# A float32 attention and FFN kernel on one core: the second FFN product of chunks 4 to 6 on two levels of Strassen's scheme, weights of chunks 3 to 6 converted in chunks 2 and 3, two-term sums through PSUM copies

## The chip, the cores and the metric

The kernel runs on one core of a Trainium2 chip, one launch, all arithmetic on the device. The metric is the device time of a run in microseconds (us): 2410.17 as the median of three runs, 2409.39 to 2412.51.

## The reference, cut to what matters

Talking-heads attention is followed by a Fourier mixing layer and a two-layer FFN with a residual. Batch 8, 12 heads, 448 positions, head size 64; so 3584 tokens of 768 numbers.

```
scores = scale * q @ k^T                      # per head
scores = mix heads with w_pre; softmax over j; mix heads with w_post
x  = attn @ v                                 # (8, 448, 768)
u  = x + real(fft over tokens and features of x)
un = (u - mean(u)) / sqrt(var(u) + 1e-6)
ch = max(un @ w_ch1, 0) @ w_ch2               # (768 x 3072), then (3072 x 768)
return u + ch
```

The two FFN weights come as float64 and are turned into float32 on the device with integer operations on VectorE.

## The kernel before

The first part, attention and Fourier mixing, takes 855.6 us; the change doesn't touch its code. The second part, `ffn_phase`, is the FFN. It cuts the 3072 hidden columns into NC = 6 chunks of 512 and the 3584 tokens into NTB = 7 blocks of 512, and runs 42 passes: pass n has chunk c = n // 7 and block t = n % 7. The text counts chunks from 1 to 6, so chunk 4 starts with pass 21.

Both products of a pass are computed with one level of Strassen's scheme in Winograd's form: seven products of half-size matrices for eight. `first(n)` (from L966) does un @ w_ch1: seven products, each of 6 matmuls of 128x128 weights by 256 columns, in the order `ORDER` = 0, 4, 5, 1, 6, 2, 3. The combinations of un and of the weights are prepared ahead: those of un in `total` (L962), which stores all seven for later chunks (`ub_scr`), those of the weights by the class `_Weights`. The results are summed as they come: products 0, 5, 6 and 3 accumulate in one PSUM tile P, 4 and 2 in R, 1 in Q. Sums of two terms that lie in different tiles are made by copying the first to SBUF (ScalarE, L990 to L994) and adding the second to it (VectorE, L996, L999, L1002), with the ReLU after it on ScalarE (L997, L1000, L1003, L1005). Then come the combinations of the hidden tile h that the next product needs: `hs1` = h21 + h22 (L1020), `hs2` = hs1 - h11 (L1021), h21 = h11 - h21 (L1022).

`second(n, h)` (from L1025) multiplies h with the chunk's part of w_ch2: seven products, each of 4 matmuls (two row halves by two hidden halves) of 128x128 weights by 384 columns. In chunk 1 the sums are added to u (L1049). In later chunks they are made in an SBUF tile `od` by copies on ScalarE (L1058) and sums on VectorE (L1060), and each finished quarter is added to the output in memory by a DMA with accumulation, issued by GpSimd (L1062). h12 - hs2 is made in place after product 1 (L1065).

Matmuls are float32: the trace shows each as two records, with a weight load (LDWEIGHTS) each.

The order on TensorE and VectorE is the order of the program text (`tc.manual_schedule`); in `ffn_phase` the other engines' and the DMA queues' order is the scheduler's. [...] PSUM has two tiles for each of P, Q and R, and from pass 1 a third for P and R (`ps_tile`). h has one buffer (`ph`), the combinations of un have eleven (`pub`).

Weights of chunk c + 1 are converted during chunk c. `_Weights.add` queues a part: four pieces of seven VectorE operations each (L235 to L261), four combining sums (L267), loads (L213) and stores (L221) by GpSimd's DMA queue. `deal(k)` lets the next k VectorE operations out; it stands after the products of both functions with 3 and 4. A chunk has five parts, one each in five of its seven passes, and `deal(1000)` at the end of a pass lets out the rest. SyncE loads the converted weights (`load_w1`, `load_w2`) in the last pass of a chunk, each as soon as its buffer is free, and the next pass's un combinations (`new_ub`) through all passes.

Of the kernel before, what the change touches and what calls it, by code (L numbers as in the profile page):

```python
# [837 lines left out]
OPENS = (0, 1, 4)  # L838
DEST = {0: (0, 0), 1: (0, 0), 4: (1, 1), 5: (0, 1), 2: (0, 1), 6: (1, 1), 3: (1, 0)}
# [4 lines left out]
def ffn_phase(ctx, tc, rest, ident, u_scr, u_rev, wts, ub_scr, out, fold_rest,  # L844
# [15 lines left out]
    pw2 = pool("pw2", 7)  # L860
# [23 lines left out]
    us, ubs, w1, w2 = {}, {}, {}, {}  # L884
    pd = []
# [24 lines left out]
    def load_w2(c, i):  # L910
        w2[i] = pw2.tile([P, FM, DH], F32, name="w2t", tag="w2t")
        nc.sync.dma_start(out=w2[i][:, :, :], in_=wts.w2[c][i])
# [57 lines left out]
    def first(n):  # L970

        c, t = divmod(n, NTB)
        h = ph.tile([P, 6, FM, HT], F32, name="h", tag="h")

        h11, h12, h22, h21, hs1, hs2 = (h[:, x] for x in range(6))
        norms = c == 0 and t + 1 < NTB
        ps = {}
        for k, i in enumerate(ORDER):
            if i in OPENS:
                ps[ACC[i]] = ps_tile(ACC[i])  # L980
            p = ps[ACC[i]].rearrange("p (m t) -> p m t", m=FM)
            ub = ubs.pop((n, i))
            for m in range(FM):
                for kc in range(NK):
                    nc.tensor.matmul(p[:, m, :], w1[i][:, kc, m * P:(m + 1) * P],  # L985
                                     ub[:, kc, :],
                                     start=i in OPENS and m == kc == 0,
                                     stop=kc == NK - 1, skip_group_check=True)
            if i == 0:
                nc.scalar.copy(out=h11, in_=p)  # L990
            elif i == 4:
                nc.scalar.copy(out=h22, in_=p)
            elif i == 5:
                nc.scalar.copy(out=h21, in_=p)  # L994
            elif i == 1:
                nc.vector.tensor_tensor(h11, h11, p, op=ALU.add)  # L996
                nc.scalar.activation(h11, h11, ACTF.Relu)  # L997
            elif i == 6:
                nc.vector.tensor_tensor(h22, h22, p, op=ALU.add)  # L999
                nc.scalar.activation(h22, h22, ACTF.Relu)  # L1000
            elif i == 2:
                nc.vector.tensor_tensor(h21, h21, p, op=ALU.add)  # L1002
                nc.scalar.activation(h21, h21, ACTF.Relu)  # L1003
            else:
                nc.scalar.activation(h12, p, ACTF.Relu)  # L1005
            if norms and k < NT2:
                stats(t + 1, k)
                if k == NT2 - 1:
                    power(t + 1)
            if n == 0 and k not in (1, 2):  # L1010
                next_part()
            if i != 2:
                wts.deal(2 if norms else 3)
            if t == NTB - 1 and c + 1 < NC:
                load_w1(c + 1, i)
            if NTB <= n + 1 < NC * NTB:
                new_ub(n + 1, i)
                nc.sync.dma_start(out=ubs[n + 1, i][:, :, :],
                                  in_=ub_scr[(n + 1) % NTB][i])
        nc.vector.tensor_tensor(hs1, h21, h22, op=ALU.add)  # L1020
        nc.vector.tensor_tensor(hs2, hs1, h11, op=ALU.subtract)  # L1021
        nc.vector.tensor_tensor(h21, h11, h21, op=ALU.subtract)  # L1022
        return h

    def second(n, h):  # L1025
        c, t = divmod(n, NTB)
        h11, h12, h22, hs3, hs1, hs2 = (h[:, x] for x in range(6))
        lhs = (h11, h12, h12, h22, hs1, hs2, hs3)
# [7 lines left out]
        for k, i in enumerate(ORDER):  # L1036
            for x in range(NT2 // 2):
                if i in OPENS:
                    ps[ACC[i], x] = ps_tile(ACC[i])
                p = ps[ACC[i], x][:, :DH]  # L1040
                for kf in range(FM):
                    nc.tensor.matmul(p, lhs[i][:, kf, x * P:(x + 1) * P],  # L1042
                                     w2[i][:, kf, :], start=i in OPENS and kf == 0,
                                     stop=kf == FM - 1, skip_group_check=True)
                r, d = DEST[i]
                last = i in (1, 6, 2, 3)
                if c == 0:
                    us_ = u[:, 2 * r + x, d * DH:(d + 1) * DH]
                    nc.vector.tensor_tensor(us_, us_, p, op=ALU.add)  # L1049
                    if last:  # L1050
                        r0 = t * TB + (2 * r + x) * P
                        nc.sync.dma_start(out=acc[t, r, d][:, x, :], in_=us_)
                    continue
                if (r, d) not in os:
                    os[r, d] = pd[0].tile([P, 2, DH], F32, name="od", tag="od")
                o = os[r, d][:, x, :]
                if i in (0, 4, 5, 3):
# [6 lines left out]
            if i == 1:  # L1064
                nc.vector.tensor_tensor(h12, h12, hs2, op=ALU.subtract)  # L1065
# [8 lines left out]
            wts.deal(2 if norms and k >= NT2 else 4)  # L1074
            if t == NTB - 1 and c + 1 < NC:
                load_w2(c + 1, i)
# [11 lines left out]
    with tc.manual_schedule(engines={ET.PE, ET.DVE}):  # L1088
# [7 lines left out]
        for n in range(NC * NTB):  # L1096
            c, t = divmod(n, NTB)

            if c + 1 < NC and 0 <= t - (c == 0) < NK + FM:
                wts.add(c + 1, t - (c == 0))  # L1100
            wts.deal(0)
            if c == 0 and t + 2 < NTB:
                load_u(t + 2)
            second(n, first(n))
            wts.deal(1000)
            if n == 0:
                assert not parts
                rest.close()
                pd.append(pool("pd", 6, side="right"))
                beside.close()  # L1110
                pps.append(pool("ppy", space=bass.MemoryType.PSUM))

# [60 lines left out]
```

## Time and profile before

| | |
|---|---|
| median of three runs | 2410.17 us (2409.39 to 2412.51) |
| the profiled execution | 2417.4 us, its span 2415.6 us |
| first pass starts | at 855.6 us |
| pass 0; passes 1 to 5 | 49.1 us; 39.9 us each |
| passes 6 to 40 | 36.19 us each: 18.13 us first product, 18.06 us second |
| from the last pass's second product to the end of the span | 26.8 us |
| DMA share in chunks 2 to 5; chunk 6 | 0.73 to 0.74; 0.54 |

A row of the profile gives line, engine, operation, operands with shape, number, busy time and the mean of one in ns. Records of pipelined matmuls overlap, so a row's mean (379 ns for 128x256) is longer than the distance between two of them (216 ns); where pace matters, the starts are read. PEld is the weight load. A part of the trace is asked for by a window in us from the start of the span.

### The profile page before, as it was taken

To read this page: it belongs to the slowest core of one execution; us is meant where nothing else is said; L and a number is where in the kernel's file an instruction comes from. 1 tells how busy PE (TensorE), PEld (TensorE's weight loads), DVE (VectorE), ACT (ScalarE), POOL (GpSimd) and SP (SyncE) were. 2 spreads that over 40 slices of the span, in tenths; PEclk is the share of its full clock that TensorE was granted. 3 is DMA by queue.
4 is the path that set the end of the run, shared out by engine and by line. 5 is a ranking of instruction groups with operands and counts; after the bars stand their busy time and mean duration, and the time that the engine had idled before them with its cause. 6 is when DMAs were issued, how large, how long until landed. Compare 5 with 4: busy or idle time off the path is not lost.

```text
span 2415.6 us, 55276 instructions
## 1 busy us (share of the span) xinstructions
PE 2363.0 (98%) x21680; PEld 1592.6 (66%) x21680; DVE 1408.6 (58%) x2859; ACT 932.7 (39%) x2335; POOL 960.3 (40%) x1395
## 2 busy tenths in 40 slices
PE   6999999999999999999999999999999999999998
PEld 2555555555555577677777777777777777777775
DVE  3888888888887767775555255624552455421221
ACT  4777777666667532231222222222222222222221
POOL 3587877868776541210223023212222223111111
PEclk9999999999999999999999999999999999999999
DMA  7565555655554565658687677777686777585453
GB/s 160 163 179 167 183 172 166 190 162 180 169 164 157 165 248 184 213 180 308 165 198 187 182 201 171 197 184 201 173 205 149 221 190 188 137 232 112 108 115 53
DMA packets 207184, 427.59 MB, mean 177 GB/s; under 512 B 38990, under 2 KB 128870, under 8 KB 206926
## 3 DMA queue, kind: packets, MB, share of 16 engines
q1 hardware_dynamic: 129902, 261.60, 32.4%
q0 software_dynamic: 71456, 161.08, 31.1%
q8 instruction: 173, 2.83, 0.5%
q10 hardware_dynamic: 5568, 1.38, 0.4%
q14 instruction: 85, 0.70, 0.1%
HBM read 211.98 MB, written 129.39 MB: 141 GB/s over the span
## 4 chain that ended last, share of the span: by engine, by line
PE 77%; issue 11%; DMA 4%; DVE 2%; POOL 2%; ACT 1%; SPq 1%; POOLq 0%; ACTq 0%; DVEq 0%
PE psP L985 15%; PE psP L1042 14%; PE psR L985 7%; PE psR L1042 7%; PE mx L486 6%; PE ms L459 5%; PE ms L547 5%; PE po L520 5%; PE psQ L1042 4%; PE psQ L985 4%; DMA Kr<-Sb 3%; POOL out_dram L1062 2%; PE ms L661 2%; PE ms L434 1%; SPq L475 1%
## 5 line engine op out<-in xcount | busy, mean ns | idle before, releaser
L985 PE MATMUL psP<-ub,w1t 128*128 128x256 f32 x2016 | 462.5, 379 | 0.0
L1042 PE MATMUL psP<-w2t,h 128*128 128x384 f32 x1344 | 460.9, 486 | 0.0
L985 PEld LDWEIGHTS psP<-ub,w1t 128*128 128x128 f32 x2016 | 382.8, 190 | 60.7
L1062 POOL DMA_DIRECT2D out_dram<-od x140 | 170.9, 1221 | 590.5 <-DVE od L1060 467.7
L1042 PEld LDWEIGHTS psP<-w2t,h 128*128 128x128 f32 x1344 | 254.4, 190 | 165.9
L510 POOL TENSOR_SCALAR PP<-PP,rcp 128x448 f32<-128x448 f32 x384 | 253.8, 670 | 230.0 <-DVE rcp L508 201.2
L500 ACT ACTIVATE PP<-mx,nmx 128x448 f32<-128x448 f32 x384 | 240.7, 632 | 174.4 <-DVE nmx L493 162.9
L493 DVE TENSOR_REDUCE nmx<-mx 128x1 f32<-128x448 f32 x384 | 223.0, 617 | 94.4 <-PE mx L486 92.5
L213 POOL DMA_DIRECT2D raw<-in_moe_w_ch_dram x120 | 72.6, 605 | 515.1 <-DVE tmp L257 507.7
L1058 ACT COPY od<-psP 128x384 f32<-128x384 f32 x210 | 100.6, 479 | 437.1 <-PE psP L1042 437.1
L486 PE MATMUL mx<-Kr,kw 60*32 60x448 f32 x3072 | 236.4, 552 | 17.2 <-DMA Kr<-Sb 13.7
L996 DVE TENSOR_TENSOR h<-h,psQ 128x512 f32<-128x512 f32 x42 | 28.9, 687 | 381.3 <-PE psQ L985 381.3
L985 PE MATMUL psR<-ub,w1t 128*128 128x256 f32 x1008 | 231.3, 379 | 0.0
L1042 PE MATMUL psR<-w2t,h 128*128 128x384 f32 x672 | 230.5, 486 | 0.0
L531 DVE STREAM_TRANSPOSE Pv<-po 128x896 f32<-128x896 f32 x192 | 212.6, 1107 | 9.0 <-PE po L520 6.1
L520 PE MATMUL po<-PP,kw 60*32 60x448 f32 x3072 | 214.2, 543 | 3.4 <-POOL PP L510 1.8
L459 PE MATMUL ms<-kT,qT 64*32 64x448 f32 (+1 forms) x3072 | 207.2, 547 | 7.3 <-ACT qT L330 6.4
L985 PEld LDWEIGHTS psR<-ub,w1t 128*128 128x128 f32 x1008 | 191.4, 190 | 25.9
L330 ACT COPY Sb<-ms 124x448 f32<-124x448 f32 x384 | 184.0, 542 | 36.7 <-DMA Kr<-Sb 16.1
L547 PEld LDWEIGHTS ms<-Pv,vv 64*64 64x64 f32 x5376 | 144.5, 133 | 70.5 <-issue 37.3
L1042 PEld LDWEIGHTS psR<-w2t,h 128*128 128x128 f32 x672 | 127.2, 190 | 87.4
L547 PE MATMUL ms<-Pv,vv 64*64 64x120 f32 x5376 | 167.8, 269 | 1.0 <-issue 1.0
(101 smaller groups left out, 2925.0 us busy)
## 6 DMA issues: line engine op xcount, KB each, us to landing
ub<-ub SPq DMA_DIRECT2D x294, 384.0 KB
Kr<-Sb SPq DMA_DIRECT2D x768, 105.0 KB
out_dram<-od POOLq DMA_DIRECT2D x140, 384.0 KB, 6.3
raw<-in_moe_w_ch_dram POOLq DMA_DIRECT2D x72, 256.0 KB, 3.8
raw<-in_moe_w_ch_dram POOLq DMA_DIRECT2D x48, 384.0 KB, 3.7
w<-wst POOLq DMA_DIRECT2D x126, 128.0 KB, 3.5
w<-wst POOLq DMA_DIRECT2D x84, 192.0 KB, 3.5
w1t<-w SPq DMA_DIRECT2D x42, 384.0 KB
```

Source lines behind the costliest of these rows:

```text
L330: (nc.scalar.copy if eng == "a" else nc.vector.tensor_copy)(out=out, in_=in_)
L459: nc.tensor.matmul(pss[x][o:o + hi - lo, :S], st["qT", xx][64 * x:64 * x + 64, y, lo:hi], st["kT", xx][64 * x:64 * x + 64, y, :], start=Tr ...
L486: nc.tensor.matmul(mx[x][64 * z + o:64 * z + o + 32, :S], kw1[64 * x:64 * x + KR, o:o + 32], Kr[64 * x:64 * x + KR, z, :], start=True, sto ...
L493: nc.vector.tensor_reduce(nmx[:, :], steps[T]["mx"][x][:, :S], axis=AX.X, op=ALU.max, negate=True)
L500: nc.scalar.activation(steps[T]["PP"][:, x, :], steps[T]["mx"][x][:, :S], ACTF.Exp, bias=steps[T]["nmx", x][:, :], accum_out=steps[T]["den ...
L510: nc.gpsimd.tensor_scalar(PP[:, x, :], PP[:, x, :], rcp[:, x:x + 1], 1.0, op0=ALU.mult, op1=ALU.mult)
L520: nc.tensor.matmul(po[o:o + 32, z, :S], kw2[64 * z:64 * z + KR, y, :], PP[64 * z:64 * z + KR, :, c * HS:(c + 1) * HS], start=True, stop=True)
L531: nc.vector.transpose(g["Pv"][:, T % GT, :].rearrange("p (z s) -> p z s", z=2), steps[T]["po"][:, :, :S])
L547: nc.tensor.matmul(pss[y][64 * x:64 * x + 64, :nu * R], st["v", pr][64 * y:64 * y + 64, x, jb * D:(jb + 1) * D], _ap(Pv, 64 * y * rp + 32 ...
L985: nc.tensor.matmul(p[:, m, :], w1[i][:, kc, m * P:(m + 1) * P], ub[:, kc, :], start=i in OPENS and m == kc == 0, stop=kc == NK - 1, skip_g ...
L1042: nc.tensor.matmul(p, lhs[i][:, kf, x * P:(x + 1) * P], w2[i][:, kf, :], start=i in OPENS and kf == 0, stop=kf == FM - 1, skip_group_check ...
L1062: nc.gpsimd.dma_start(out=acc[t, r, d], in_=os[r, d][:, :, :], accum_op=ALU.add)
```

## The change

In chunks 4 to 6 (`DEEP` = 3), `second` is replaced by `second2`: each of its seven products (256 x 256 by 256 x 384) is again made of seven, on 128 x 128 weights by 192 columns, 49 matmuls in all. The combinations of the left side are made by `quarter`: for h11 and h22, and for h12 and h12 - hs2, on GpSimd, for h21, hs1 and hs2 on VectorE; those of the right side by `halves`, once in a chunk, in turn on VectorE and GpSimd. The matmuls of three neighbouring products are interleaved by steps: product j starts at step 7j, and its matmuls m = 0, 4, 5, 1, 6, 2, 3 stand at 0, 3, 4, 5, 8, 13 and 16 after it. Steps from 49 on run among the next pass's first product (`SEAM`), and the first matmul of step 0 runs before the last two matmuls of `first`. ScalarE takes results out of PSUM (`take`) and copies a first term into another PSUM tile (`begin`), where the second is accumulated by the matmul without its start flag. VectorE adds (`more`) and joins products (`both`); each output quarter leaves by one DMA with accumulation, and in the last pass one quarter by two. In chunks 4 to 6 ScalarE's and GpSimd's order is that of the text too.

In `first` from pass 9 on, and in `second` from chunk 2 on, the sum of products 0 and 1 is made the same way, by a ScalarE copy of P into Q. h12 - hs2 has its own place in h and is made before the second product. The weights of chunks 3 and 4 are converted in chunk 2, those of 5 and 6 in chunk 3, and unfinished conversions of these chunks go on into the next pass. w2 has a buffer for each of the seven products, `od` seven buffers for six.

```diff
+ORDER2 = (0, 3, 5, 6, 4, 1, 2)
+DEEP = 3
+CONV = ((1, 2, 3), (2, 4, 5))
...
-    pw2 = pool("pw2", 7)
+    pw2 = pool("pw2")
...
+    H11, H22, H21, HS1, HS2, H12, H12S = range(7)
+    LHS = (H11, H12, H12S, H22, HS1, HS2, H21)
...
+    def quarter(eng, hq, h, f0, f1, s):
+        o = hq[:, f0:f1, :, :]
+        a11, a12, a21, a22 = (h[:, f0:f1, f, x * P:(x + 1) * P]
+                              for x in range(2) for f in range(2))
+        to, a, b, op = ((o[:, :, 0], a21, a22, ALU.add),
+                        (o[:, :, 1], o[:, :, 0], a11, ALU.subtract),
+                        (o[:, :, 2], a11, a21, ALU.subtract),
+                        (o[:, :, 3], a12, o[:, :, 1], ALU.subtract))[s]
+        eng.tensor_tensor(to, a, b, op=op)
+    def halves(i, eng):
+        wt[i] = right["wt"].tile([P, 3, DQ], F32, name="wt", tag=f"wt{i}")
+        b11, b12 = w2[i][:, 0, :DQ], w2[i][:, 0, DQ:]
+        b21, b22 = w2[i][:, 1, :DQ], w2[i][:, 1, DQ:]
+        t1, t2, t4 = (wt[i][:, x, :] for x in range(3))
+        for to, a, b in ((t1, b12, b11), (t2, b22, t1), (b12, b22, b12), (t4, b21, t2)):
+            eng.tensor_tensor(to, a, b, op=ALU.subtract)
...
+        deep = c >= DEEP
+        seed = n >= NTB + 2
...
+            if deep and t == 0:
+                halves(ORDER2[k], (nc.vector, nc.gpsimd)[k % 2])
...
+                    for fn in beside.pop(done, ()):
+                        fn()
+                    done += 1
...
-                                     start=i in OPENS and m == kc == 0,
+                                     start=i in (0, 4, 1)[:3 - seed] and m == kc == 0,
...
+            if i == 0 and seed:
+                ps["Q"] = ps_tile("Q")
+                nc.scalar.copy(out=ps["Q"][:, :], in_=ps["P"][:, :])
...
+            elif i == 1 and seed:
+                nc.scalar.activation(h11, p, ACTF.Relu)
...
+                if deep:
+                    for x in range(4):
+                        quarter(nc.gpsimd, hq, h, H11, H22 + 1, x)
...
+            if i == 2:
+                vec.tensor_tensor(hs1, h21, h22, op=ALU.add)
+                vec.tensor_tensor(hs2, hs1, h11, op=ALU.subtract)
+                vec.tensor_tensor(h21, h11, h21, op=ALU.subtract)
+                if deep:
+                    for x in range(4):
+                        quarter(vec, hq, h, H21, HS2 + 1, x)
...
-        nc.vector.tensor_tensor(hs1, h21, h22, op=ALU.add)
-        nc.vector.tensor_tensor(hs2, hs1, h11, op=ALU.subtract)
-        nc.vector.tensor_tensor(h21, h11, h21, op=ALU.subtract)
-        return h
-    def second(n, h):
+        vec.tensor_tensor(h12s, h12, hs2, op=ALU.subtract)
+        if deep:
+            for x in range(4):
+                quarter(nc.gpsimd, hq, h, H12, H12S + 1, x)
...
-                if i in (0, 4, 5, 3):
+                if i == 0:
+                    q = ps["Q", x] = ps_tile("Q")
+                    nc.scalar.copy(out=q[:, :DH], in_=p)
+                elif i in (4, 5, 1, 3):
...
-            if i == 1:
-                nc.vector.tensor_tensor(h12, h12, hs2, op=ALU.subtract)
...
+    def second2(n, st):
+        c, t = divmod(n, NTB)
...
+        def mm(j, m):
+            i = ORDER2[j]
+            h, hq = st["h"][:, LHS[i]], st["hq"][:, LHS[i]]
+            key = {0: "P", 5: "P", 6: "P", 3: "P", 4: "R", 2: "R", 1: "Q"}[m]
+            if m in (0, 4):
...
+            a = {0: h[:, 0, :P], 1: h[:, 1, :P], 3: h[:, 1, P:], 4: hq[:, 0], 5: hq[:, 1],
+                 6: hq[:, 2], 2: hq[:, 3]}[m]
+            b = {0: w2[i][:, 0, :DQ], 1: w2[i][:, 1, :DQ], 2: w2[i][:, 1, DQ:],
+                 3: wt[i][:, 2], 4: wt[i][:, 0], 5: wt[i][:, 1], 6: w2[i][:, 0, DQ:]}[m]
+            nc.tensor.matmul(ps[j, key][:, :DQ], a, b, start=m in (0, 4), stop=True,
+                             skip_group_check=True)
...
+        def take(j, q, key):
+            nc.scalar.copy(out=part(j, q), in_=ps[j, key][:, :DQ])
+        def begin(j):
+            ps[j, "Q"] = ps_tile("Q")
+            nc.scalar.copy(out=ps[j, "Q"][:, :DQ], in_=ps[j, "P"][:, :DQ])
+        def more(j, q, key):
+            vec.tensor_tensor(part(j, q), part(j, q), ps[j, key][:, :DQ], op=ALU.add)
+        def both(eng, j, k):
+            eng.tensor_tensor(D[j][:, :, :], D[j][:, :, :], D[k][:, :, :], op=ALU.add)
+        def out_(j, r, d):
+            nc.gpsimd.dma_start(out=acc[t, r, d], in_=D[j][:, :, :], accum_op=ALU.add)
...
+        for j, i in enumerate(ORDER2):
+            b = 7 * j
+            for s, m, q, key in ((0, 0, None, None), (3, 4, 3, "R"), (4, 5, 1, "P"),
+                                 (5, 1, None, None), (8, 6, None, None),
+                                 (13, 2, None, None), (16, 3, 2, "P")):
+                on(b + s, mm, j, m)
+                if m == 0:
+                    on(b + s, begin, j)
+                if key:
+                    on(b + s, take, j, q, key)
+            on(b + 6, take, j, 0, "Q")
+            on(b + 11, more, j, 3, "P")
+            on(b + 16, more, j, 1, "R")
             if t == NTB - 1 and c + 1 < NC:
-                load_w2(c + 1, i)
+                on(b + 17, load_w2, c + 1, i)
+        j0, j3, j5, j6, j4, j1, j2 = range(7)
+        for j, ops in ((j5, ((j5, j0),)), (j6, ((j6, j5), (j3, j6))),
+                       (j4, ((j6, j4), (j5, j4))), (j1, ((j0, j1),))):
+            for o in ops:
+                on(7 * j + 19, both, vec, *o)
+        on(7 * j6 + 20, out_, j3, 1, 0)
+        on(7 * j4 + 20, out_, j6, 1, 1)
+        on(7 * j1 + 20, out_, j0, 0, 0)
+        if n < NC * NTB - 1:
+            on(7 * j2 + 19, both, vec, j5, j2)
+            on(7 * j2 + 20, out_, j5, 0, 1)
+        else:
+            on(7 * j4 + 20, out_, j5, 0, 1)
+            on(7 * j2 + 19, out_, j2, 0, 1)
+        return at
...
+        parts_ = [(0, 1, k) for k in range(NK + FM)]
+        parts_ += [(c, d, k) for c, *ds in CONV for d in ds for k in range(NK + FM)]
+        for n in range(DEEP * NTB):
             c, t = divmod(n, NTB)
-            if c + 1 < NC and 0 <= t - (c == 0) < NK + FM:
-                wts.add(c + 1, t - (c == 0))
+            for _ in range((0 < t < NK + FM + 1) if c == 0 else 2 if t < 3 else 1):
+                if parts_ and parts_[0][0] == c:
+                    wts.add(*parts_.pop(0)[1:])
...
+            if c == 0 or t == NTB - 1:
+                wts.deal(1000)
...
+    SEAM = {49: 0, 50: 1, 51: 1, 52: 1, 53: 2, 54: 2, 55: 3, 56: 3, 57: 4, 58: 5, 59: 5}
+    with tc.manual_schedule(engines={ET.PE, ET.DVE, ET.Activation, ET.Pool}):
+        rest_ = {}
+        for n in range(DEEP * NTB, NC * NTB):
+            st = {}
+            at = second2(n, st)
+            beside = {}
+            for s_ in sorted(rest_):
+                beside.setdefault(SEAM.get(s_, s_ - 54), []).extend(rest_[s_])
+            beside.setdefault(NK * FM * 7 - 2, []).extend(at.pop(0))
+            first(n, st, beside)
+            rest_ = {}
+            for s_ in sorted(at):
+                if s_ < 49:
+                    for fn in at[s_]:
+                        fn()
+                else:
+                    rest_[s_] = at[s_]
```

## The prediction

> Passes are numbered 0 to 41: chunk 1 holds 0 to 6, chunks 4 to 6 hold 21 to 41. Times are us unless marked ns.
>
> **What bounds the kernel now.** I read the page, the windows by pass, then the timelines of single passes.
>
> ```profile
> span 2415.6 us, 55276 instructions
> PE 2363.0 (98%) x21680; PEld 1592.6 (66%) x21680; DVE 1408.6 (58%) x2859; ACT 932.7 (39%) x2335; POOL 960.3 (40%) x1395
> ```
> ```profile
> 1393.50:1429.70 36.20, 36.20 (x141) 26.60 (x140) 18.94 (x47) 8.08 (x15) 11.18 (x15) 1.00 0.72 194
> ...
> 1574.50:1610.70 36.20, 36.20 (x142) 26.61 (x141) 7.98 (x13) 8.08 (x15) 4.79 (x4) 1.00 0.57 127
> 1610.70:1646.80 36.10, 36.10 (x141) 26.55 (x140) 9.55 (x18) 8.08 (x15) 4.81 (x4) 1.00 0.88 248
> ```
> TensorE is bound. After each window stand length, then busy PE, PEld, DVE, ACT and POOL, clock, DMA share, GB/s. In passes 14, 19 and 20 PE is busy throughout at full clock; the others are far from full. Pass 14 converts weights, 19 doesn't, 20 loads the next chunk's.
>
> A busy PE proves little, so I check its pace:
> ```profile
> 1662.38 2.75 PE L985 MATMUL psP<-ub,w1t 128*128 128x256 f32 x12
> 1664.97 2.74 PE L1042 MATMUL psP<-w2t,h 128*128 128x384 f32 x8
> 1667.55 2.74 PE L1042 MATMUL psR<-w2t,h 128*128 128x384 f32 x8
> ```
> Products start 2.59 and 2.58 apart: 12 records of 215.8 ns, 8 of 322.5. A float32 matmul has two records, each with a weight load. A pass is 18.13 + 18.06 = 36.19, and passes 6 to 40 all start 36.19 apart: no bubble to save. Only less PE work helps.
>
> **What the Trainium skill says.** "TensorE: Matmul & The Clock Gate", section Back-to-back issue gap: N/2.4 + 2.5 ns. With two passes over the columns in a record it gives 215.8 and 322.5 ns, as the trace has; for N = 192 it gives 162.5. Its section LDWEIGHTS says columns/1.2, so 107 ns for 128. The trace agrees:
> ```profile
> 889.87 0.82 PE L952 MATMUL psQ<-ident,un 128*128 128x128 f32 x6
> 890.52 1.48 PE L661 MATMUL ms<-tcs,z 97*113 97x193 f32 x8
> 891.83 2.74 PE L1042 MATMUL psQ<-w2t,h 128*128 128x384 f32 x8
> ```
> Six transposes with 128 weight columns in 0.65: 108 ns each. Eight records of 192 or 193 columns in 1.31: 164 ns. So weight loads hide under narrow matmuls too, though the row of a load shows 190 ns.
>
> "SBUF — State Buffer", section Who interferes with whom: a VectorE instruction with two SBUF inputs and a GpSimd one that reads SBUF exclude each other for the whole instruction. The trace agrees:
> ```profile
> L267 DVE TENSOR_TENSOR wst<-wst x120: 404/426/2728, 164.7 to 2075.2; 128x256 f32<-128x256 f32 x72, 128x384 f32<-128x384 f32 x48
> L615 POOL TENSOR_TENSOR xq<-xs x64: 579/594/1304, 138.1 to 861.5; 113x192 f32<-113x192 f32 x32, 113x191 f32<-113x191 f32 x32
> ```
> The 2728 ns of L267 (minimum/median/maximum) lie where GpSimd ran sums back to back.
>
> "PSUM — Partial Sum Buffer", The four PSUM rules: a ScalarE write leaves the accumulate bits alone, so a matmul adds onto a copied seed where an earlier matmul set the bit. No trace here shows that; it touches the result, not the time.
>
> **Part 1, second product on two levels, passes 21 to 41.** 28 matmuls of 384 columns go, 49 of 192 come: 98 x 162.5 ns = 15.93 for 56 x 322.5 = 18.06. Gain 2.13 a pass, 44.8 in 21.
>
> New side work in a pass. ACT: 35 copies of 192 columns at 0.32 (L1058 479 ns for 384, L330 211 for 60), with the first product's some 15.5 of 34.1. DVE: fourteen 192-column sums at 0.355, seven `both` at 0.95 (L964), `quarter` four at 0.55, six 512-column sums at 0.69: 18. POOL: eight `quarter` sums of 256 columns at 0.73 (between L615 594 ns for 192 and L601 1001 for 384), four output DMAs at 1.21: 10.7. None is full, so it is a question of order. In the steady part each wait has slack: a small product's m=6 follows its m=5 by four matmuls (1.30), while m=5's own 0.33, 0.20 until ACT sees its end, the copy of 0.32 and 0.16 to restart make 1.0. DVE falls 0.3 behind at the double `both` and the waiting m=3 has over 0.8.
>
> **Part 2, the turn from first to second product.** Put 0 at the end of `first`'s last matmul. The product i=2 ended at -2.92 (after it come six wide matmuls of 0.43 and one narrow of 0.33). The chain after it is in pass 41 of the trace:
> ```profile
> 2386.38 0.69 DVE L1002 TENSOR_TENSOR h<-h,psR 128x512 f32<-128x512 f32 x1 [1.83 <-PE psR L985]
> 2387.10 0.63 ACT L1003 ACTIVATE h<-h 128x512 f32<-128x512 f32 x1 [1.89 <-DVE h L1002]
> 2387.76 0.69 DVE L1020 TENSOR_TENSOR h<-h 128x512 f32<-128x512 f32 x1 [0.70 <-ACT h L1003]
> 2388.49 0.69 DVE L1021 TENSOR_TENSOR h<-h 128x512 f32<-128x512 f32 x1
> ...
> 2389.10 0.68 DVE L1022 TENSOR_TENSOR h<-h 128x512 f32<-128x512 f32 x1
> ```
> From i=2's end (2386.18) to the end of L1022 is 3.61: now at +0.69. Behind it on DVE stand four `quarter` (two dependent, 0.03 gaps; two overlapping by 0.08: to 2.79), `h12s` (to 3.40) and only then the first `more` (3.31 to 3.67). For that sum waits m=3 of the first small product, the twelfth matmul: due at 11 x 0.325 = 3.58. Behind it on PE is everything. A matmul that waited for L959's copy began 0.05 after it and lost 0.10 of prefetch, so it runs at 3.83: bubble 0.25. Then the port: POOL's `quarter` of H11 and H22 runs from -3.81 to -0.86 (i=6 ends at -5.51, sum and relu of H22 by -3.89, then four of 0.73), and DVE's `hs1`, due at -1.33, has two SBUF inputs. It waits 0.47, of which some 0.12 overlaps its start: +0.35. I take 0.6 a pass: 12.6 (bounds 0.25 to 0.8: 5 to 17).
>
> In the first pass of chunks 4, 5, 6 `halves` comes too: four DVE sums of 0.35 ahead of `h12s` (1.2) and four on POOL right behind `quarter`, which hold the port against `hs1` and `hs2` for up to 2.4. I take 3.5 x 3 = 10.5 (0 to 12).
>
> **Part 3, conversions moved.** Chunks 2 and 3 carry two chunks' worth each: 46 operations dealt a pass instead of 32, dealt as densely as before, but with no rest. DVE: 46 at about 0.45 = 20.5 and 6.3 of sums, 27 of 36.2. Its sums are early in either half, with over 1 us to spare before PE needs P again. Each raw load and wst store moves along, on POOL's queue among the output DMAs: 5.8 x 0.6 + 10 x 0.6 + 4 x 1.21 = 14. DMA: a part costs 0.18 of a pass's share (0.74 mean with, 0.57 without); 1.44 parts make 0.83, but passes 13 and 20 also load weights (+0.31): 1.14, that is 5 us too much. `ub` loads are issued a pass early, so I cost this at 1 (0 to 8; without that cover 5 each). In chunks 5 and 6 DVE and queues are relieved, which PE didn't wait for: nothing.
>
> In pass 20 DVE's order puts the first `halves` ahead of that pass's own sums; they wait for w2 loads, which are issued as the products end, the fifth at 13 of `second`, and take some 4 (the 384 KB raw loads land after 3.7). Sums due at 13 come at about 17, and PE's i=3, due at 15.5, waits: 3 (0 to 6; below nothing excluded, since nothing is removed there).
>
> **Part 4, sums by PSUM copies.** An ACT copy at i=0 is used two products later; the DVE sum at i=1 goes. PE waits for neither: 0.
>
> **Part 5, the tail.** Now the last DMA is issued 1.0 after the last matmul ends:
> ```profile
> 2407.81 1.19 POOL L1062 DMA_DIRECT2D out_dram<-od  x1 [1.24 <-ACT od L1058]
> ```
> and lands 6.1 later. After, the last two DMAs add to the same block, so the second waits for the first (issued near 17 of `second2`, after the last double `both`, landing at 23); it lands at 29 to 30. With 1.6 after it: 31, where before 26.8 followed `second`'s start. Pass 41's 2.13 is in the gain already, so the cost is the tail's growth from 8.7 to 14: 5 (3 to 6).
>
> **Sum.** 44.8 - 12.6 - 10.5 - 1 - 3 - 5 = 12.7. The profiled execution, 2417.4 (span 2415.6), would become 2404.7; it lies 7.2 above the median of the runs. On the median, 2410.2 - 12.7 = 2397.5.
>
> **Rivals.**
> A, the forecast: 2397.5, own range 2388 to 2405. Chance 0.45.
> B, the port costs nothing, the turn only 0.25 and 1.2: 44.8 - 5.3 - 3.6 - 5 = 31: 2379. For it: overlaps of L261 with GpSimd in which it still took 404 ns. Against: `quarter` reads two SBUF inputs, as the rows that blocked did. 0.25.
> C, chunks 2 and 3 pay: raw loads late behind output DMAs, DVE stalls, passes 13 and 20 lose 5 each: 2407. Against: 36.19 a pass at 0.88 DMA share. 0.17.
> D, slower: POOL's `quarter` is longer than I think. Each us past -0.86 goes one for one into the turn. At 1.0 a sum (L601's) it ends at +0.25, the bubble is 1.7, 36 in all, with 19.5 of the rest: 2421. It decides from a bubble of 1.2. Against: L615 and L601 bracket 256 columns. 0.10.
> E, weight loads don't hide: 98 x 190 ns = 18.6, more than before: 2430 or more. Against: 108 ns. 0.03.
>
> About 0.2% (4.8) can be told from no change. Faster: A, B and a little of C, 0.75; within: 0.12; slower: D, E, 0.13. The range reaches from B to beyond C: 2377 to 2409.
>
> **What would show it.** Passes 21 to 40 start about 34.7 apart (B 34.3, D over 36); narrow records 162 to 164 ns; in each pass one PE gap some 3.5 after `first`, ended by a 192-column DVE sum into od; `hs1` some 0.35 longer than 688 ns; passes 21, 28, 35 longest; passes 7 to 19 still 36.19; the last DMA some 6 after the one before it. Wrong if PE waits for ACT throughout `second2`, or if passes 7 to 20 stretch.

## The result, and the profile after

| | before | after |
|---|---|---|
| median of the runs (us) | 2410.17 (11 runs, 2404.54 to 2419.14) | 2399.41 (11 runs, 2391.20 to 2406.53) |
| profiled execution (span) | 2417.4 (2415.6) | 2406.5 (2404.8) |
| start of pass 0 in the profile | 855.57 | 854.16 |
| from there to the end | 1560.05 | 1550.60 |

The ratio is 0.9958, 95% interval 0.9941 to 0.9974: faster, by 10.8 us on the medians where 12.7 was forecast. All that stands ahead of pass 0 is the same code in every kernel here, and takes 844 to 856 us from one profiled run to the next. So I compare what follows the first matmul of pass 0: 9.45 less. That is one profiled execution against one; the medians come from 11 runs each.

The page of after, PE first. It is still busy for almost the whole span, with less work to do:
```profile
span 2404.8 us, 58524 instructions
PE 2325.9 (97%) x22562; PEld 1703.2 (71%) x22562; DVE 1601.5 (67%) x3244; ACT 1090.0 (45%) x2930; POOL 1107.1 (46%) x1600
```
Four passes of after as windows: 15, 20, 22 and 28. The columns are the length, busy PE, PEld, DVE, ACT and POOL, the clock, the DMA share and GB/s.
```profile
1429.83:1466.02 36.19, 36.19 (x141) 26.60 (x140) 22.68 (x57) 8.96 (x17) 12.04 (x18) 1.00 0.78 196
1610.78:1651.70 40.92, 38.16 (x142) 27.33 (x141) 27.85 (x66) 8.96 (x17) 10.53 (x16) 0.96 0.96 304
1687.44:1722.14 34.70, 34.47 (x184) 31.83 (x183) 17.06 (x32) 15.00 (x43) 10.61 (x13) 1.00 0.55 126
1895.70:1932.78 37.08, 34.48 (x185) 31.81 (x183) 26.19 (x48) 14.99 (x43) 19.16 (x25) 1.00 0.54 141
```
Pass 15 converts weights for two chunks and still takes 36.19. Pass 20, the last of chunk 3, takes 4.7 more. Pass 22 is what a deep pass (one with `second2`) costs, 34.70; pass 28, a first pass of a chunk, has 2.4 more, and DVE and POOL are each 9 busier in it. PE is busy throughout in pass 15 and nearly so in 22; no other engine is near full in any of the four; in pass 20 the DMA share is 0.96.

The starts of all passes, taken from the first matmul of each, give this list (36.19 is the length before). Passes 22 to 27, 29 to 34 and 36 to 40 are the 17 ordinary deep passes.

| passes | length after (us) |
|---|---|
| 6 to 13, 15 to 19 | 36.19 |
| 14 | 37.74 |
| 20 | 40.91 |
| 21 | 35.75 |
| 22 to 27, 29 to 34, 36 to 40 | 34.69 to 34.75 |
| 28, 35 | 37.08, 38.54 |
| 41 to the end | 51.73 (before: 44.98) |

The pace inside the second product, from the timeline of pass 22. Each row is one matmul of 192 columns, two records:
```profile
1716.94 0.49 PE L1149 MATMUL psQ<-w2t,h 128*128 128x192 f32 x2
1717.27 0.49 PE L1149 MATMUL psR<-w2t,hq 128*128 128x192 f32 x2
1717.59 0.49 PE L1149 MATMUL psP<-w2t,h 128*128 128x192 f32 x2
```
They start 0.325 apart, 162.5 ns a record: TensorE follows its own pace there, and no weight load shows.

The turn from the first to the second product in pass 24, timeline of DVE, POOL and PE:
```profile
1773.68 0.73 POOL L985 TENSOR_TENSOR hq<-hq,h 128x256 f32<-128x256 f32 x1
...
1773.88 0.69 DVE L1046 TENSOR_TENSOR h<-h,psR 128x512 f32<-128x512 f32 x1 [1.80 <-PE psR L1021]
...
1775.05 0.75 POOL L985 TENSOR_TENSOR hq<-h,hq 128x256 f32<-128x256 f32 x1
1775.27 1.08 DVE L1059 TENSOR_TENSOR h<-h 128x512 f32<-128x512 f32 x1 [0.70 <-ACT h L1047]
1776.38 0.69 DVE L1060 TENSOR_TENSOR h<-h 128x512 f32<-128x512 f32 x1
...
1779.71 0.68 DVE L1071 TENSOR_TENSOR h<-h 128x512 f32<-128x512 f32 x1
...
1780.31 0.35 DVE L1165 TENSOR_TENSOR od<-od,psP 128x192 f32<-128x192 f32 x1
...
1780.71 0.59 PE L1149 MATMUL psP<-wt,h 128*128 128x192 f32 x2 [0.23 <-DVE od L1165]
```
`hs1` (L1059) starts while POOL's last quarter sum runs and takes 1.08 where `hs2`, of the same form, takes 0.69. The sum just before it (L1046), whose second input lies in PSUM, runs beside POOL sums of the same kind for its whole length and loses nothing: 0.69. At the end of the chain the matmul waits for the first `more` (L1165). By the starts of the records, TensorE's gap there is 0.39, and the next record starts 0.10 later than its pace; this second part is called restart below.

### The profile page after: what moved, and what is told of

The parts are those of the page before. It is cut to its first block, busy times and chain, and to the rows that moved or that the text cites. A ratio compares the mean times of both kernels' runs of the same rounds, so it can differ in the third digit from the quotient of the medians.

```text
span 2404.8 us, 58524 instructions
## 1 busy us (share of the span) xinstructions
PE 2325.9 (97%) x22562; PEld 1703.2 (71%) x22562; DVE 1601.5 (67%) x3244; ACT 1090.0 (45%) x2930; POOL 1107.1 (46%) x1600
## 4 chain that ended last, share of the span: by engine, by line
PE 79%; DVE 7%; DMA 6%; issue 3%; ACT 2%; POOL 1%; SPq 1%; POOLq 0%; DVEq 0%; ACTq 0%
PE psP L1021 15%; PE psR L1021 9%; PE psP L1093 8%; PE mx L486 6%; PE psP L1149 6%; PE ms L459 5%; PE ms L547 5%; PE po L520 5%; PE psQ L1021 4%; PE psR L1093 4%; PE psR L1149 3%; DMA Kr<-Sb 3%; PE psQ L1093 2%; DVE hq L985 2%; PE ms L661 2%
## 5 line engine op out<-in xcount | busy, mean ns | idle before, releaser
L1021 PE MATMUL psP<-ub,w1t 128*128 128x256 f32 x2016 | 475.9, 379 | 1.3 <-DVE h L1040 1.3
L510 POOL TENSOR_SCALAR PP<-PP,rcp 128x448 f32<-128x448 f32 x384 | 254.7, 673 | 229.2 <-DVE rcp L508 199.9
L1093 PE MATMUL psP<-w2t,h 128*128 128x384 f32 x672 | 232.3, 489 | 2.8 <-DVE od L1113 2.8
L1171 POOL DMA_DIRECT2D out_dram<-od x85 | 103.1, 1230 | 213.4 <-ACT od L1158 161.4
L1040 DVE TENSOR_TENSOR h<-h,psP 128x512 f32<-128x512 f32 x42 | 28.9, 687 | 252.1 <-PE psP L1021 251.8
L985 POOL TENSOR_TENSOR hq<-h 128x256 f32<-128x256 f32 x84 | 61.4, 731 | 276.3 <-issue 170.6
L1093 PEld LDWEIGHTS psP<-w2t,h 128*128 128x128 f32 x672 | 127.4, 191 | 85.1 <-DVE od L1113 3.7
L1168 DVE TENSOR_TENSOR od<-od 128x768 f32<-128x768 f32 x146 | 137.6, 954 | 35.3 <-ACT od L1158 34.3
L221 POOL DMA_DIRECT2D w<-wst x210 | 129.1, 648 | 50.6 <-DVE wst L267 22.3
```

The costliest lines, as they stand in the source:

```text
L510: nc.gpsimd.tensor_scalar(PP[:, x, :], PP[:, x, :], rcp[:, x:x + 1], 1.0, op0=ALU.mult, op1=ALU.mult)
L1093: nc.tensor.matmul(p, h[:, LHS[i], kf, x * P:(x + 1) * P], w2[i][:, kf, :], start=i in (0, 4, 1)[:3 - (c > 0)] and kf == 0, stop=kf == FM ...
```

## Experiments

Each kernel is the changed kernel with one edit, unless said otherwise. "From pass 0" is the time from its first matmul to the end of the span in the profile; after has 1550.60. Each ratio is to the kernel before in the same session, from 4 to 20 runs.

| kernel | median | ratio to before, 95% | from pass 0 |
|---|---|---|---|
| h12s behind the first `more` | 2387.4 | 0.9902 (0.9879 to 0.9925) | 1538.80 |
| POOL's quarter off `hs1` | 2387.9 | 0.9920 (0.9892 to 0.9947) | 1540.33 |
| one POOL sum twice | 2412.0 | 1.0004 (0.9994 to 1.0015) | 1565.70 |
| halves earlier | 2390.8 | 0.9920 (0.9893 to 0.9947) | 1539.86 |
| conversions and copies alone | 2411.8 | 1.0002 (0.9987 to 1.0016) | 1563.34 |
| halves pinned behind pass 20 | 2396.4 | 0.9946 (0.9933 to 0.9959) | 1544.27 |
| conversions dealt faster | 2395.0 | 0.9944 (0.9922 to 0.9965) | 1542.85 |
| one DMA at the end | 2398.6 | 0.9949 (0.9937 to 0.9962) | 1548.23 |
| four edits | 2374.9 | 0.9859 (0.9835 to 0.9883) | 1524.08 |
| five edits | 2376.1 | 0.9846 (0.9823 to 0.9870) | 1522.31 |
| five, and the relu later | 2379.9 | 0.9865 (0.9843 to 0.9887) | 1526.63 |

My theory is the forecast's: the turn is DVE's order and the shared port, and the single losses are places where DVE or POOL has something put ahead. The rivals were that the port costs nothing, that chunks 2 and 3 pay for the conversions, and that another engine ends at the same time, so that nothing is gained.

### DVE's order at the turn

```diff
-        vec.tensor_tensor(h12s, h12, hs2, op=ALU.subtract)
-        if deep:
-            for x in range(4):
-                quarter(nc.gpsimd, hq, h, H12, H12S + 1, x)
+        if not deep:
+            vec.tensor_tensor(h12s, h12, hs2, op=ALU.subtract)
...
+        def late():
+            h = st["h"]
+            vec.tensor_tensor(h[:, H12S], h[:, H12], h[:, HS2], op=ALU.subtract)
+            for x in range(4):
+                quarter(nc.gpsimd, st["hq"], h, H12, H12S + 1, x)
...
+        on(12, late)
```
Step 12 lies behind the first `more`, at step 11.

> Edit: in chunks 4 to 6 the sum h12s and POOL's four quarter sums of H12 and H12S are issued after the first 192-column DVE sum (more) of the second product instead of before it; nothing is left out. Theory A (DVE's order makes the turn): h12s stood ahead of that sum with a pitch of 0.60 us, and the gap was 0.39 + 0.10, so an ordinary deep pass falls from 34.70 to 34.2 apart, the gap of some 2.74 in passes 21, 28 and 35 falls by 0.60, and the whole by 18 x 0.49 + 3 x 0.60 = 10.6. Rival (TensorE waits there for something else that ends at the same time: ScalarE's copies or GpSimd): passes stay at 34.70 and the time does not move.

Passes 22 to 27, 29 to 34 and 36 to 40 are 34.20 apart, 0.50 less; pass 28 fell by 0.60 to 36.48. From pass 0 it is 11.8 less where 10.6 was expected; 1.2 of that is pass 20, which no part of the edit touches and which takes 39.6 to 42.8 in the kernels that leave it as it is. The timeline of pass 24 of this kernel:
```profile
1770.31 0.35 DVE L1163 TENSOR_TENSOR od<-od,psP 128x192 f32<-128x192 f32 x1
1770.57 0.68 DVE L1173 TENSOR_TENSOR h<-h 128x512 f32<-128x512 f32 x1
...
1770.93 0.49 PE L1147 MATMUL psP<-wt,h 128*128 128x192 f32 x2
```
The sum that TensorE needs (L1163) now runs ahead of `h12s` (L1173), and the matmul has no wait. `h12s` itself is needed six small products later. So the gap is DVE's order; the rival, another engine that ends at the same time, falls.

### The shared port

```diff
             elif i == 1 and seed:
                 nc.scalar.activation(h11, p, ACTF.Relu)
+                if deep:
+                    for x in range(4):
+                        quarter(nc.gpsimd, hq, h, H11, H11 + 1, x)
...
-                        quarter(nc.gpsimd, hq, h, H11, H22 + 1, x)
+                        quarter(nc.gpsimd, hq, h, H22, H22 + 1, x)
```


> Edit: POOL's four quarter sums over H11 and H22 together (256 columns, 0.73 each, which overlap DVE's hs1) become four of H11 alone right after its relu and four of H22 alone after its relu (128 columns each); h12s stays where it is; nothing is left out. Theory A (SBUF port): H22's four end some 1.2 us earlier, ahead of hs1, which falls from 1.08 to 0.69 us; everything behind it on DVE is 0.39 earlier, the gap of 0.39 + 0.10 a pass goes or nearly goes, passes fall from 34.70 to 34.2 to 34.3, the whole by 8 to 10. Rival B (the port costs nothing, hs1 is long for another reason): hs1 stays at 1.08 and the passes at 34.70.

The passes are 34.32 apart. The same place in pass 24 of this kernel:
```profile
1763.62 0.46 POOL L985 TENSOR_TENSOR hq<-h,hq 128x128 f32<-128x128 f32 x1
1764.71 0.69 DVE L1062 TENSOR_TENSOR h<-h 128x512 f32<-128x512 f32 x1 [0.70 <-ACT h L1050]
```
POOL ends 0.63 ahead of `hs1` (here L1062), which takes 0.69. The 0.39 that it lost was the port's, and came off the pass one for one: 34.70 to 34.32; 0.10 of restart stays, since the sum now ends just in time. Rival B falls. A general slowness of DVE beside POOL falls too: L1046 lost nothing. From pass 0 it is 10.3 less where 8 to 10 was expected. Either edit alone takes all or most of the 0.49, because both shorten the same chain.

For the slope, one of the four POOL sums was made twice:
```diff
-                    for x in range(4):
+                    for x in (0, 1, 2, 2, 3):
                         quarter(nc.gpsimd, hq, h, H11, H22 + 1, x)
```


> Edit: the changed kernel with one of POOL's four quarter sums of H11 and H22 (0.73 us) made twice, with the same result; nothing is left out. This measures the slope of rival D of the prediction. If each us of POOL goes one for one into the turn, as put there, DVE's hs1 waits for all of it, the gap grows from 0.39 to 1.1, ordinary passes from 34.70 to 35.4, and the kernel is 15 us slower than without the edit and no faster than before the change. If the two engines take turns at the port, sum by sum, as the first passes of the chunks hint (five DVE sums beside four on POOL lost 1.5), DVE loses some 0.3 to 0.4: passes at 35.0 to 35.1, 7 us. If the port costs nothing: 34.70.

```profile
1768.61 1.19 DVE L1059 TENSOR_TENSOR h<-h 128x512 f32<-128x512 f32 x1 [0.69 <-ACT h L1047]
1769.21 1.18 POOL L985 TENSOR_TENSOR hq<-h,hq 128x256 f32<-128x256 f32 x1
1769.84 1.10 DVE L1060 TENSOR_TENSOR h<-h 128x512 f32<-128x512 f32 x1
```
In pass 24 of it `hs1` waits for a POOL sum, the last POOL sum (1.18, not 0.73) waits for `hs1`, and `hs2` waits for that. From the start of L1059 to the start of L1061 it is 2.25 us, in the changed kernel 1.72: DVE loses 0.53 for 0.73 of POOL, and ordinary passes are 35.22 to 35.25 apart, 0.53 more. So the slope is 0.7, between my two cases: the engines take turns. "SBUF — State Buffer", section Who interferes with whom, calls the port that the two share an exclusive lock, which agrees; one for one, as the prediction had it, is only the upper end. From pass 0 the kernel is 15.1 slower than without the edit, which looks like one for one and isn't: 9.0 lie in the 17 ordinary passes; 5.1 in passes 21, 28 and 35, of which 2.0 are longer gaps and 3.1 are TensorE at half clock in places where it wasn't before; and pass 20, which the edit doesn't touch, takes 1.3 more. The median is that of before. TensorE's losses in an ordinary pass add up to 1.17 here, and the prediction had put the point from which rival D decides at 1.2.

### Halves in the first passes

```diff
-                halves(ORDER2[k], (nc.vector, nc.gpsimd)[k % 2])
+                for j in ((0,), (1,), (2, 3), (4, 5), (6,), (), ())[k]:
+                    halves(ORDER2[j], (nc.vector, nc.gpsimd)[j % 2])
```


> Edit: in the first pass of chunks 4, 5 and 6 the halves sums of the last products are issued two products earlier (DVE's last at the fifth product instead of the seventh, POOL's last at the fourth instead of the sixth); nothing is left out. Theory A: no halves stand between hs1 and the first more on DVE or hold the port then, so the gaps of 2.74 to 2.77 in passes 21, 28 and 35 fall to the 0.4 of other passes, 2.4 each, 7 in all, and some 1.1 more where TensorE ran slow after the gap in pass 35: 8. Pass 20 keeps its 4.7, ordinary passes 34.70. Rival (the first pass is late for its weights or its ub): the three gaps stay above 2.

Passes 28 and 35 are both 34.66 now, pass 21 33.32. Together that is 8.7 less, where 8 was expected. In the changed kernel the turn of pass 28 is:
```profile
1914.13 1.02 DVE L1059 TENSOR_TENSOR h<-h 128x512 f32<-128x512 f32 x1 [0.70 <-ACT h L1047]
1914.54 1.06 POOL L994 TENSOR_TENSOR wt<-w2t 128x192 f32<-128x192 f32 x1
...
1919.76 0.34 DVE L994 TENSOR_TENSOR wt<-w2t 128x192 f32<-128x192 f32 x1
...
1921.95 0.59 PE L1149 MATMUL psP<-wt,h 128*128 128x192 f32 x2 [2.60 <-DVE od L1165]
```
Four POOL sums of `halves` lie beside DVE's five sums from L1059 on; from its start to the start of the third quarter sum DVE takes 4.69, in this experiment 3.47:
```profile
1902.27 1.04 DVE L1060 TENSOR_TENSOR h<-h 128x512 f32<-128x512 f32 x1 [0.70 <-ACT h L1048]
...
1905.74 0.55 DVE L985 TENSOR_TENSOR hq<-h 128x384 f32<-128x384 f32 x1
...
1907.68 0.59 PE L1150 MATMUL psP<-wt,h 128*128 128x192 f32 x2 [0.19 <-DVE od L1166]
```
DVE's own four `halves` sums take 1.19. 1.22 + 1.19 is the 2.4 that went from pass 28; pass 35 fell by another 1.46, since TensorE no longer ran at half clock after its gap. The rival (late weights or ub) falls: nothing was loaded earlier.

### Conversions and copies alone

```diff
-DEEP = 3
+DEEP = 6
```
(with a guard for the last chunk's w2 load.)

> Edit: the second product stays on one level in all chunks, so that of the change only the moved conversions and the two-term sums by PSUM copies remain; nothing is left out. Theory A: passes 7 to 13 and 15 to 41 lie 36.19 apart, pass 14 alone is some 1.5 longer (the DMA engines are full through passes 13 and 14), pass 20 loses nothing without halves, and the tail is as before the change: 1 to 2 us slower than before, a ratio of 1.000 to 1.001. Rival C (chunks 2 and 3 pay for the moved conversions): passes 7 to 20 stretch and the whole is 7 to 12 us slower. If the copies paid in themselves, passes 21 to 41 would be shorter than 36.19.

Passes 6 to 13 and 15 to 40 are 36.19, all of them; pass 14 is 40.12, that is 3.93 more, and no other pass pays. From pass 0 it is 3.3 slower than before, and the medians can't be told apart. So rival C is wrong but for one pass, and the copies cost and gain nothing in a pass; the last pass to the end is 0.64 shorter than before. Pass 14 differs from run to run with the same conversions: 36.80 to 40.12 over the kernels that deal them as the change does.

What pass 14 waits for, from the DMA page of the stretch 1385 to 1412 of the changed kernel and its timeline:
```profile
DMA  9999999999999999999999999999999999998667
```
```profile
1407.35 0.29 DVE L243 TENSOR_SCALAR wst<-tmp 128x256 uint32<-128x256 uint32 x1 [10.01 <-DMA w<-wst]
```
Each digit is a slice of 0.675 us in tenths: the DMA engines are busy for 0.9 or more in 24 us without a break, from the end of pass 13 into pass 14, where raw loads, stores and the next chunk's weights meet. Three stores of converted pieces issued from 1391.8 to 1392.9 take 9.1 to 9.4 us to land; two at 1420.9 and 1421.5 take 2.6 and 2.5. A store lands so late that DVE stands for 10 us before it may write that buffer again, and behind this conversion stands the sum (L1040) that TensorE needs.

### Dealing the conversions faster

```diff
-            for _ in range((0 < t < NK + FM + 1) if c == 0 else 2 if t < 3 else 1):
+            for _ in range((0 < t < NK + FM + 1) if c == 0 else (2, 2, 2, 2, 1, 1, 0)[t]):
...
-                wts.deal(2 if norms else 3)
+                wts.deal(2 if norms else 4)
```


> Edit: conversions in chunks 2 and 3 are dealt four instead of three DVE operations after each product of the first half, and two parts are begun in each of the first four passes, so that they are over before the last pass of the chunk; nothing is left out. Theory A (pass 14 is longer because the DMA engines are full through passes 13 and 14, where weight loads meet raw loads and stores, and the store of a converted piece lands late): pass 14 falls from 37.7 to 36.2, which is 1.5 us, if passes 7 to 12 bear four operations a product; each product has 2.59 us and four operations take 1.8. Rival (the denser dealing itself makes DVE late): passes 7 to 12 and 14 to 19 stretch by 0.1 to 1 each.

Pass 14 is 36.19, pass 10 36.56, pass 17 36.22. Theory A holds for pass 14, and the rival has the 0.4 of pass 10. What the edit takes away is the load of the DMA engines and the piece that DVE waits with, both at once. And pass 20 fell from 40.91 to 36.19 as well, which I had not expected of it.

### Pass 20

```diff
-            eng.tensor_tensor(to, a, b, op=ALU.subtract)
+            op = eng.tensor_tensor(to, a, b, op=ALU.subtract)
+            if i == 0 and to is t1:
+                tc.keep_in_program_order(op)
```


> Edit: the first halves sum of pass 21 is pinned on DVE behind everything that pass 20 issues there; nothing else is touched and nothing is left out. Theory A (DVE's order: halves that wait for w2 loads stand ahead of pass 20's own sums): TensorE's gap of 2.9 us in pass 20 and the slow records behind it go, pass 20 falls from 40.9 to 36.2, and passes 21, 28 and 35 stay as they are: 4 to 5 us in all. Rival (pass 20 is late because its DMA engines are overloaded with weight loads, or its conversions fill DVE): pass 20 stays above 39.

Pass 20 is 36.19, though the DMA share in it is 1.04 (second number from the end) and all its conversions are there:
```profile
1607.14:1643.33 36.19, 36.19 (x142) 26.60 (x141) 26.38 (x57) 8.95 (x17) 11.90 (x17) 1.00 1.04 330
```
The rivals (DMA, DVE full of conversions) fall as causes by themselves. In the changed kernel it looks so:
```profile
1640.60 0.36 DVE L994 TENSOR_TENSOR wt<-w2t 128x192 f32<-128x192 f32 x1 [5.38 <-DMA w2t<-w]
...
1646.72 0.55 DVE L1113 TENSOR_TENSOR od<-od,psP 128x384 f32<-128x384 f32 x1
...
1647.32 4.54 PE L1093 MATMUL psP<-w2t,h 128*128 128x384 f32 x8 [2.76 <-DVE od L1113]
```
DVE stands 5.4 us before the first of `halves`, for its w2 load; then it works off 6.1 us of conversions and further `halves` that had piled up, and only then comes L1113, for which TensorE waits. Without the halves in front (pinned, or none at all in the kernel with conversions alone) the wait is gone. It is gone too where conversions are dealt faster, though there the halves still stand in front and wait 6.3 us for their w2 load. It takes both.

### One DMA at the end

```diff
-        if n < NC * NTB - 1:
-            on(7 * j2 + 19, both, vec, j5, j2)
-            on(7 * j2 + 20, out_, j5, 0, 1)
-        else:
-            on(7 * j4 + 20, out_, j5, 0, 1)
-            on(7 * j2 + 19, out_, j2, 0, 1)
+        on(7 * j2 + 19, both, vec, j5, j2)
+        on(7 * j2 + 20, out_, j5, 0, 1)
```


> Edit: in the last pass the last product is added into the sum before it on DVE and leaves with it in one output DMA, as in all other passes, instead of two DMAs of which the second adds to the block of the first; nothing is left out. Theory A (the second DMA waits for the first to land): the last DMA is issued near 1.8 us after the last 192-column sum starts instead of 7.8, one DVE sum of 0.95 comes in, and the stretch from the start of pass 41 to the end falls from 51.7 by about 5 to 46.7. Rival (DMAs add to memory at a rate that four in a row have used up, so that the last lands as late as before): it falls by less than 2.

From pass 41 to the end it is 47.90, 3.8 less: most of the 5, not all. The changed kernel's last DMA:
```profile
2390.24 0.35 DVE L1165 TENSOR_TENSOR od<-od,psR 128x192 f32<-128x192 f32 x1
2398.07 1.20 POOL L1171 DMA_DIRECT2D out_dram<-od  x1 [5.92 <-DMA out_dram<-od]
```
And that of this kernel:
```profile
2388.14 0.35 DVE L1165 TENSOR_TENSOR od<-od,psR 128x192 f32<-128x192 f32 x1
2390.18 1.20 POOL L1171 DMA_DIRECT2D out_dram<-od  x1 [0.46 <-issue]
```
The last one no longer waits for an earlier DMA into the same block to land, and is issued 2.0 after the last small sum's start instead of 7.8. But from its issue to the end of the span it is 8.6, with the other 6.7: four output DMAs of 384 KB went out between 2385.1 and 2391.4, and the DMA engines were busy with them for 10.5 us, 2.6 each. So the rival has a share of 1.9.

### Together

The four edits are `h12s` later, halves earlier, the pin, and one DMA.

> Edit: four edits together, h12s and its quarter sums after the first more, halves two products earlier, the first halves pinned behind pass 20, one output DMA at the end; nothing is left out. Theory A: the gains add up, as each takes away another wait: passes 22 to 40 at 34.20 (8.5 for ordinary ones), passes 21, 28 and 35 at 32.8, 34.2 and 34.2 (10.2), pass 20 at 36.2 (4.7), the end 5.7: 29 less than the changed kernel from the first pass to the end, 1521.5 instead of 1550.6, some 2371 in all, and a ratio of 0.983 to 0.985 to the kernel before. Rival (a wait that stood behind these takes their place, ScalarE's copies above all): passes stay above 34.4 and less than 22 is gained.

Passes 22 to 40 are 34.20, every one, pass 21 32.90, pass 20 36.19. 26.5 from pass 0 where 29 was expected: pass 14 happened to take 38.61, and the end fell by 4.1 instead of 5.7.

> Edit: the four edits of e8_four and the denser dealing of conversions of e7_parts together; nothing is left out. Theory A: pass 14 falls from 38.6 to 36.2, pass 10 rises by 0.4, the rest stays: 2 us less than e8_four from the first pass to the end, so 1522, some 2373 in all, a ratio of 0.984 to 0.986 to the kernel before. Rival: with conversions out of pass 20 the pin makes the halves late, and pass 21 grows by more than 1.

Pass 14 went to 36.19 and pass 10 to 36.88; 1.8 less from pass 0. On the clock the two can't be told apart. Both beat the change by 1.0 to 1.1%, and the kernel before by 1.4 to 1.5%.

> Edit: e10_five, and ScalarE's relu of h12 is issued after the first two 192-column copies (take) of the second product instead of before them; nothing is left out. What is left of the turn are 0.074 before the sixth small matmul and 0.074 of restart, which waits for the second of those copies. Theory: the relu (0.60) ahead of them on ScalarE makes that copy late, so 0.15 a pass goes: passes at 34.05, 3 us in all, some 2370. Rival (the copy starts as soon as its matmul has ended, so the distance of two matmuls is too short in itself, or the relu now delays the copies behind it): passes stay at 34.20 or above.

```diff
-            else:
-                nc.scalar.activation(h12, p, ACTF.Relu)
+            elif deep:
+                st["p12"] = p
...
+        def relu12():
+            nc.scalar.activation(st["h"][:, H12], st["p12"], ACTF.Relu)
...
+            if j == 0:
+                on(5, relu12)
```
A miss. The passes are 34.37, 0.17 longer. The gap ahead of the sixth small matmul shrank from 0.074 to 0.014, but its restart of 0.074 stayed, and 0.118 and 0.104 came up two matmuls later, behind the delayed copies. The rival is right, in its second form: the turn's rest isn't worth a change of ScalarE's order.

## Why the prediction was right, and where not

The forecast was 1.9 us off on the median, the direction right. By the prediction's own steps, from pass 0 to the end in the profiled pair, where it was 3.3 off:

| step | forecast | measured |
|---|---|---|
| TensorE's work, 21 passes | -44.8 | -44.8 |
| the turn | +12.6 | +13.5 |
| first passes of chunks 4, 5, 6 | +10.5 | +8.6 |
| conversions | +1 | +1.6 |
| pass 20 | +3 | +4.7 |
| the tail | +5 | +6.9 |
| sum | -12.7 | -9.45 |

- **Work.** 98 records of 162.5 ns, as forecast for 192 columns; loads hide (rival E falls).
- **Turn.** 21 x 0.645. The chain forecast 0.25, with 0.10 of restart in it, and 0.35 for the port. It measures 0.49, with 0.39 from the port. Right chain, some 0.1 too much in all. The other 0.15 is a wait the forecast ruled out: it reckoned that m=6 has 1.3 and needs 1.0, which holds in the steady part, but at the first small product ScalarE still has its relu of h12 in front, and the copy ends 0.074 late (without the relu in front it is 0.014; the restart stays).
- **First passes.** 2.35 + 2.38 + 3.84 over an ordinary pass (pass 21 is 1.30 shorter than others by nature, as the four edits show: 32.90 to 34.20, since no small matmuls of a pass before lie in it). Both parts of the mechanism hold, 1.19 on DVE and 1.22 at the port, where up to 2.4 was put: again the engines take turns. So what the forecast had in mind cost 7.1 of its 10.5. The other 1.46, in pass 35, is TensorE at half clock, which the forecast didn't have.
- **Conversions.** The overload was named and placed, and the pass right behind it paid, though a stretched pass from 7 to 20 stood among the signs of being wrong; but what was late wasn't a ub load, it was a buffer held by its store.
- **Pass 20.** Named, with the waiting halves, though by the same sign pass 20 shouldn't have stretched at all. Too small, because the sum stood behind the conversions that piled up during the wait too, and because TensorE ran slow for a while afterwards.
- **Tail.** 51.73, less what pass 41 should take: 44.98 - 2.13 + 0.645 + 1.30 = 44.80. Of the 6.9, the second DMA's wait is the greatest part (3.8 come back without it); 0.88 is a wait of TensorE for a `more` behind two `both` in the last pass, where no matmuls of a next pass fill in. The forecast didn't have that, and it put 6 for the landing of the DMA that the last one waits for, which took 8.2. Its sum had a slip as well: from its 31 and 26.8 the growth is 31 - 26.8 + 2.13 = 6.3, or 5.7 if the 31 holds the turn's 0.6, and it wrote 5.

One reading of before was loose: beside the 2728 ns of L267 GpSimd ran two TENSOR_SCALAR (L510) and one two-input sum (L606), not sums alone.

So rival A, the forecast, is what happened. The gain was exact; four costs were too small by 0.6 to 1.9 each and one too large by 1.9, and that one made the sum better than its terms: so much of the closeness is luck. More of it lies in the draw. With nothing changed in them, pass 14 takes 36.80 to 40.12 in these kernels, pass 20 39.55 to 42.80, passes 28 and 35 37.05 to 38.59, so a term of 1 to 5 us that was met once isn't confirmed to a few tenths. The mechanism of the two largest costs, turn and first passes, is what the experiments show; the size of the turn was nearly right. What stays open is how the 0.6 to 3.9 of pass 14 are drawn from run to run, and what would shorten the rest of the tail: neither was tried further.

## What to carry to other kernels

When a kernel is bound by TensorE and a change trades matmuls for side sums, price the matmuls first, then list in order what each side engine has queued at the points where TensorE turns from one phase to the next: a sum that isn't needed for a long time costs up to its full length there, and moving one such sum with its four followers gave about 11 us, as much as the whole change. A wait for a load at the head of DVE's queue costs the wait and all that piles up behind it. At the end of a kernel, don't let the last output DMA add to a block which an earlier one is still writing.

## What the runs showed of the hardware

A DVE sum with both inputs in SBUF and a GpSimd sum take turns, here at a loss of 0.39 us where they overlap by 0.53; a DVE sum with one input in PSUM lost nothing over 0.69 us of overlap (pass 24 above).

TensorE may run at half clock for a while after a gap of 2 to 4 us. Pass 35 and pass 28 of the changed kernel, the stretch behind the gap, as windows with the clock as the third number from the end:
```profile
2167.37:2170.00 2.63, 2.63 (x9) 2.63 (x10) 0.32 (x2) 0.96 (x3) 2.43 (x4) 0.50 0.00 0
1922.11:1925.00 2.89, 2.89 (x19) 2.89 (x20) 1.02 (x4) 1.73 (x6) 2.44 (x4) 1.00 0.00 0
```
Both gaps were the same, 2.74 and 2.77, and only one had the slow stretch (9 records against 19 in about the same time). Over all kernels here, by the starts of the records, gaps of 2.1 to 2.9 had it in 5 of 21 cases, gaps of 3.1 to 3.9 in 5 of 8, gaps of up to 1.6 never, and it cost 1.4 to 3.0. "TensorE: Matmul & The Clock Gate", Part 1, has the clock fall after an idle window of about 3.4 us, which runs free. No run here shows the window itself. That equal gaps had it or not fits a window that runs free, but gaps from 2.1 on were enough here.
